# Attention and a cosine-gated feed-forward layer on one core: joint normalisation of two units in phases 3 to 5, with a newly searched order table

## The chip, the cores and the metric

The kernel runs on one core of a Trainium2 chip. Its time is the device time in microseconds (us) of one execution; the span is the part of it from the first to the last instruction in the trace. A core has five engines that run side by side and meet only at semaphores: PE (TensorE, matrix products into PSUM, with the weight load shown apart as PEld), DVE (VectorE), ACT (ScalarE), POOL (GpSimd) and SP (SyncE). In this kernel POOL and SP mostly issue transfers.

## The reference

The inputs are q, k and v of shape 8 x 8 x 576 x 64 (images, heads, positions, head width) and two weights, 512 x 2048 and 2048 x 512, all in float32.

```python
scores = scale * np.matmul(q, k.transpose(0, 1, 3, 2))       # scale = 1/8
bias = slopes[:, None, None] * (-np.abs(rel))[None, :, :]    # rel = position - position
mask = (rel >= 0) & (rel < 128)
attn = softmax(np.where(mask, scores + bias[None], -1e9))
x = np.matmul(attn, v)           # gathered to 4608 tokens x 512
h = x @ w_in
out = (h * np.cos(h)) @ w_out
```

## The kernel before

**Units.** Attention is cut into units: of each image (b), for two heads at a time (four pairs pr) and two halves of 256 positions (G = 0, 1), and one unit "t" for the last 64 positions of all heads: nine units an image, 72 in all. A unit has scores on PE (lines 529, 539), an exponential on ACT (590, 598), a product with the mask on DVE (611, 623) and a product with v on PE (640 to 656). The v tile has an added column of ones, so the last product also gives the sum by which the row must be divided. The norm is that division, on DVE: a reciprocal of the sums, and a product that writes 16-bit tokens, `xnats` (lines 694 and 696, function `norm`), out of the PSUM bank in which the v product stands. Afterwards the tokens are transposed into `xT`, either on PE and out of PSUM again (`x_pe`, lines 742, 752, 753) or by a transposing transfer from SP (`x_dma`, line 768). Units are handled two at a time; the v products of two units lie in PSUM banks 2 and 3.

**Two forms of norm.** Where both units of a group are ordinary ones and the phase is in the list `JN`, `norm_two` takes one reciprocal (line 710) and one product (line 712) over both banks together. Otherwise each unit has its own two instructions.

**Feed-forward.** The tokens are worked in nine chunks of 512. Chunk 0 multiplies by w_in in halves (975), chunks 1 to 5 with whole products (782), chunks 6 to 8 with sums of blocks that save one product in eight (876). The second product is plain in chunk 0 (1161) and in the block form from chunk 1 on (1067, 1138). The cosine is on ACT (787, 940, 980), its product with h on DVE (791, 943, 984).

**Phases and order.** Phase -1 has the nine units of image 0. Phases 0 to 5 stand beside the chunks of the same number and have 8, 10, 10, 12, 14 and 9 units. Every piece of work is recorded as an operation with its readers and writers; `Plan.follow` then unpacks a text, `TABLE`, into one sequence of all operations, and each engine and each queue runs its own operations in that sequence. The table also settles, where either is allowed, whether ACT or DVE copies something out of PSUM. Semaphore waits are derived from the readers and writers.

**Loads.** POOL issues the loads that change the type: q and k of images 0 and 1 in a row layout (356), v blocks (375), q and k of images 2 to 7 (385), w_in in four column quarters (407), w_out in four quarters (413). SP issues one first load of q, the transposing transfers of q and k of images 2 to 7 (396, 399), those of tokens (762, 768) and the stores of the output (1095, 1151, 1168). A load waits until its buffer is free, and what is behind it in its queue waits too.

**Start.** SP's first q load is cast by DVE and ACT (367, 368). POOL makes an identity matrix (420, 421) and the table of distances (427 to 434); ACT makes eight masks from the distances (460), and DVE widens them (465). PE transposes q and k of image 0 with the identity (483), in a first and a second part, and ACT and DVE copy them out (500, 501).

Of the kernel before, what the change touches and what calls it, by code (L numbers as in the profile page):

```python
# [8 lines left out]
ALU = mybir.AluOpType  # L9
# [5 lines left out]
B, H, S, D = 8, 8, 576, 64  # L15
NPAIR = H // 2
NBLK = 5
# [13 lines left out]
    'c-nPV2Y6If7JmPfH!Wo*A%PHdEHqifjs=k}tV#(GFqBXPBn4$bu`FK_%_4*%1ObV(K#D*JSt&-E!h-'  # L31
    '0xDvPKfD@{Z`QYO7kX6D^JciMYzU|;fHUhcd1+;jf_Kj&N_3_w#jJy552L+3%Pc;zlP#H-yktj(-'
    'pEjqM{ck}PJwCrB3q-'
    '{9M;&d$5qHR9WADS}~;_2H1xbO#`q+wdtgon`B>6%HyG|f?3%VnDsdnr<5N0St5ZZ)?8zmXNGD<Zg2=y6N`U+Gy?'
    '$F$*GyJWJoN!r+3anTS_iMU&FrmJy)q1{k##U*rYHRJHq^Dy35b!Y@oPU}o$A?_9;n<O%5Xs0l2&{m^^1BgNm_9P'
    '~pqObs4C1TN&{Qy{6(86~%nA#%H5NW^O=4`d2vLnc~h(_}2&mQcz_^`@$G{b79x#rnLjt-93Hcj0-'
    'yv%|m2e+*e0cZK}!+72b)WUaJT8@pXD+fk0N6bOV1gB(Si4?NA5T2-'
    '!JB(zEKr!Mj%{>;HUNYjab!Z7$qCql;L3G!CjefR+FFk(bw73vr<2ntCbb8MB)_5dQYyf6J%<J=0tY;ul(MgN&rc'
    'O0s&EiG$uIcm#Y~Vab;v#yqnaVrE7GY>V-A}Btqa`;P_Nv&jvF#{*7WM`>VMkre&#)Wy?uO_aV#gax-'
    'm{4=v5trFP6j>R?Tw2c0rY#J*M(j<PaOY>o)>#w^hUa2)xJ2kX>J~-'  # L40
    '#3SczLYEI#)13`0UMgZCvSU&r@KXVhQx8AYHOt^~S#t385v1pL)39f1&X4(!RY_VSn%~;N7Le~0Vt5k)3C!7qncH'
    'Sb_KKyP6<WQBL=(H{om`}^2hwehkBNkN1f6-'
    '=6Jf`#n1*9F&|{#~8ip5b`?XFO3>mnmKg4fqM&X#D2BXTu`vb#MxEL-'
    '2=FZh<=U!>)?uhVjo~ev?pC0h90j^d!W2#$W>Vg}3Lez;yMB~`dF58D5!*GHZ4bkokcrZJo8XMBIs3+J`c0!*&!='
    'cNak2M(+9t6%k<c;_TI5&xT-;_~SjMe)zLQ?kr-'
    '9G)}so_oZgT~!nS)>B%(>F{i(nL<%Kma6dPT_kIY8xqVGm@6sSZY)QY;}3kyZHF!JjrNbPWohF6A1kpQae^Jz>4Y'
    'nMq|4ag_#Z%abX$X0Qx{bdg5-'
    'w!C^Sy0wzSSv6YO*7!5g5KOZPW>L)jeqDWi^PVfHiNt_&bV&I7<#pb?el1f*R3lvbBscPqQM6(|M=#E!7MQtWiEo'
    '^$q8jetWg{{laSk`ID;w6<lHL!It@CI3ZRWxET-dy=6bdfZi^BN)-'
    'kx6rkxYh^Af7Y$CX%W0qP@nf!;+_cuy#JAV$$(>L5)aS8M@n1a32RRL3Yb{W0a`!VJ8|o4{JEnxs(L});p(&v8a9'  # L50
    'u_yO{KZHL$YuW?tu(Sy-'
    '!vCGTmAdZpg4wXLtycpkG<<E5@OtDZg=!_1h1+Njmjw*z0aL)7QnhFOPv(elHPlI>oe%EXgvk}suL+RHI+l!oPEe'
    'ttc)y)KY7q-'
    'GO9HpEp~!82*s>_!_J5TR{@5f%EL7h^Wh(4l4fbO%j~jd783&`#My06C4>3;+Is6L%3tT|^hYe#$tr1&iB&6{dwW'
    'wmj!;Baz_4=p8Jja_9ps>tY{=<;GUvOwSAXGq+K`;>!KNrH|ImXY(ASTzHFN^apdvpSj*r6^VK)$8H@P=`NPcPO&'
    'XkYSBhFw`irt0gqb!LQPqlVQC7VwU?z)4yP6n<)+6xUk=rH29r)HJ=#nkkufV0J5o_@v9wsQWd0@&P$WT0e*0vOC'
    'WIl=#9la*x}LDtWaQG=0xl2(#f%Kz3QWi+K|tR$xwKh#_K~ywPUk>V_~X988-'
    'dL$7M*|kTUzrMQ~>ttJm@GYT>9QFLiQ#JGHIu^Q5UX9joXGsV+1N~s5tf4rg&Z0t843@yK)VUZ;eO{vvf>bj#_<{'
    'E{YJE13lG{)N}UY3D6Y>lsCkRX4ja{$9_e$IQETy;j`zD56VwIGwJ{vRRhIkkY72;<?OL;WxyDsbjLJ`d?#gik4L'
    '%OwvOj>3X-Yk5pe`ia}jeHouYwjx-lYe?zUO*6w~{=z!E<7?VOdoJcyIBk3;YN22T&Udsl*?z2EoT*eN`VQ(2lOw'  # L60
    '$ie!%Cd#CND}y^H-5G~apWoVM#%(x$>q1=4UeA7@v$>FHVpXpRNz-`z1w9-2S&rNI|0<^yIkuIxJ1&2qr-'
    'yn-P&*BAkwbEg<YgZWM`B<Ux7!?;yxT0hEB9Poq9_H<xB+6$<+&1*V*jXQ=!i##UhbBC-HxJ9b4f>O5FQM$GVlYY'
    '0;EzOMeT$+Oi@ir?~G>em;QF`Fb7Uw0-'
    ')DSUv5QX5E;wvHsQX@ok50m+CO*%wR0XM0gH$JNq(o?|pd}rcrfU%@Ny^NS$EwY}9WNlRrb}CwAb0!CyUIkX8zeE'
    't`lBMNi5`Z9289jS-byN0#8`Z0-K46!6u51NJvfI*I<pVOKD}#Bep<(EjKAJ>#OvyA?}aT-'
    'Eb<QtZWG>gAiq@nZu|-Z>5YIIxXgTPJ-Qv8(%8OF{x~utj?J<T~4~q=Mu!G!`B%o{U^X7EYfMjy|cFw5l`KlR}P!'
    'Ka8_mW<8uzKs|eA|5Ic*_e7cdlcU3q+K^v!GU5I4-4igxj^A<ASLge=;<iQSZL!w7=WR?W#-'
    'vXhCLeN@7x(>g+{qRDABl6lLS<Fw>!h`LQKaFe(HMu)ipAva=P&;AW;|7_8}?>Xa&1&CWqRI3oTyJm0VHkMj~b-'
    'KU~R;VLVn(IO$x|2XD-#Cwa~YvoxGM@0FUnOnlZXB(9|3jhMQu{ARUV7(DVnyPJ@o)_f&pP-'
    '0v1&I@q5tK0fHEZqW2B6vpePz;Nsr3p!)OwvLraMQ%IB0%b!Fk8kvD!^ICX(d5SU`>)JBl;A)3x!^A~*gA1H!Njk'  # L70
    '9bb31AJ#9jLnSFn5nJP8V+>6WI*{{9$K=-'
    'Ii4(}ekB>9rlTbz8;dAV@$vsGY#Mm*p3)v9cI)0mEeyn;9Sk1Ej+_{IEB=6m(OWM%qp|L4FkV=POcUwRSz4?%tjO'
    '!EE7%nJVFo1y$1xLEKDW3+%V*`a_(LEi!<eA{Ja22J?)4@RI|7PRIIN8a6UkTIrQNx^0MmIX}Gdse33v8*ibI3(}'
    'Q6!`hQq7VFL0TWDyL%1z)LEb|Fqa2QJsRyz<9M$)jGC(Gyq6mu#GUiIyWiMn}lrw_vC^2CnX65Kq(JOA5auqsW#('
    'az6gPr;3Fs3vS*iFTO!lleCE-fW~K`s@;f-'
    'DuL7*vWwMFvwo)YDYK%Ys!&lL=}a$qa_Dqe_$j$%4|P%7Sk&C^p7|E-05OoaEoQU{w(_HKhuIl)N)0L6E?If-ndQ'
    'f>bOkomPRMj6=zXYB;2Fs8S$=8>KAS9bxj%$jo92RQykW$_h$ynL-'
    ';1n|B~0C{NjJ5M;#~HD{_qDyS92ASr8Q=(}$hf?wlN8Dh7U35CEE3Rb4eZHcVrLB=YO&ys+EVM&F9-'
    '>_E|awkyN8>TE$>Y^ZLfm%hXRv?#4)t*Y5EYzr4%5w1xWK3uw7gWYn<tfyI;9|8HRZ>;#t145fwkp%W<gb}oO8Vt'
    ';%~TDI391Zd3iT@kVuEmcuME+!AOkCeh?Xh408{MGRAGcvK=>2_;SOCz;Xi5FXBMh@##BcNK~)Hu608vNLvl*BDH'  # L80
    'GHNRFy;B3gs%n{7pj$fl+x7VWHhmHY6$LK<1t&5`BViq8BRfR0)!TR`@J<FZkbrVSDq@w=+*W79u-'
    'AsdYv9Vyey(st|R(RU84Bg0wsI(4aO|@>6G)${!)5eW-e@5K<&=Z_fWO<s>k5KMFa_g&GrXJ7L|{Z-'
    'kIjkN?mA0G*W>_y'
# [12 lines left out]
class Plan:  # L96
# [18 lines left out]
    def op(self, eng, fn, r=(), w=(), dma=None, occ=100, lat=None, pri=5, mode=0, table=None, two=False):  # L115
# [4 lines left out]
        f = fn[0] if isinstance(fn, list) else fn["act"] if isinstance(fn, dict) else fn  # L120
# [39 lines left out]
    def follow(self, text):  # L160


        raw = zlib.decompress(base64.b85decode(text))
        n, at, self.order = len(raw) // 2, 0, []
        assert n == len(self.all)
        for lo, hi in zip(raw[:n], raw[n:]):
            at = (at + lo + 256 * hi) % 65536
            o = self.all[at % 32768]
            if isinstance(o.fn, dict):
                e = "dve" if at >= 32768 else "act"  # L170
                o.fn, o.eng = o.fn[e], (e,)
            self.order.append(o)
# [80 lines left out]
def bass_alibi_sliding__then__act_gcu_kernel(  # L253
# [8 lines left out]
    with ExitStack() as ctx:  # L262
# [12 lines left out]
        JN, PRE2, SEEDN, XD, LORD = (5,), (), {}, {4: 6}, 0  # L275
# [583 lines left out]
        def moe1_fast(c, f4):  # L859
# [76 lines left out]
            def gk(hf):  # L936
                return [("g", gi, 4 * f4 + k, hf) for k in range(4)]

            def cos_and_product(src, srcs, o, cos, occ, w, r, ck, hf):
# [3 lines left out]
                op("dve", lambda e: e.tensor_tensor(o, srcs, cos, ALU.mult),  # L943
                   r=r + ck, w=w + gk(hf), occ=1139, lat=1225, pri=MPRI, two=hf == 1)
# [272 lines left out]
        distances()  # L1217
        identity()
        load_qk("q", q, 0, 1)
        load_qk("k", k, 0, 1)  # L1220
        constants()
        load_v(0, range(2))
        load_w_in(0)
        load_v(0, range(2, NBLK - LORD))
        masks()
        for n in range(2):
            qk_transposes(0, "q", n, 0, OB)
            qk_transposes(0, "k", n, 0, UB)
        for u in range(1, 4):
            load_w_in(u)  # L1230
            if u == 1:
                load_v(0, range(NBLK - LORD, NBLK))
# [92 lines left out]
```

## Time and profile before

| | |
|---|---|
| median of 3 runs (lowest, highest) | 300.07 us (299.7, 300.19) |
| the profiled execution | 299.71 us, of which 298.0 us is the span |
| granted TensorE clock in it | 1.000 |
| PE busy, share of the span | 287.9 us, 97% |
| PEld busy | 205.2 us, 69% |
| DVE busy, instructions | 262.1 us, 88%, 522 |
| ACT busy, instructions | 222.1 us, 75%, 318 |
| POOL busy | 95.2 us, 32% |
| chain that ended last, by engine | PE 94% |

Busy time is the time in which at least one instruction of the engine runs. Matrix products are pipelined: one that takes 0.38 us is followed by the next after 0.22 us, so their busy times overlap, and a short stop of PE can be hidden in them. It is seen in the distance between the starts of two products.

### The profile page before, as it was taken

The numbers are of one execution on the slowest core, as the hardware profiler recorded it, in microseconds if no ns is written. First come the engines' busy times: TensorE is split into PE (matmuls) and PEld (weight loads), VectorE is DVE, ScalarE is ACT, GpSimd is POOL, SyncE is SP. The second block draws the span as 40 slices with busy tenths as digits, with TensorE's granted clock in tenths as the row PEclk, the third lists the DMA queues.
The fourth block names the chain that finished last, engine by engine and source line by source line (L and its number), as shares of the span: only waits on it lengthen the run. The fifth ranks groups of instructions, "written<-read, shape, count | busy, mean of one in ns | idle before, by whom it ended". The sixth has DMA issues, their size and how long they took to land.

```text
span 298.0 us, 7278 instructions
## 1 busy us (share of the span) xinstructions
PE 287.9 (97%) x2974; PEld 205.2 (69%) x2974; DVE 262.1 (88%) x522; ACT 222.1 (75%) x318; POOL 95.2 (32%) x122
## 2 busy tenths in 40 slices
PE   2899999999999999999999999999999999999996
PEld 2678845446874586458854788547768888888884
DVE  3879877599977999899999999999999999999972
ACT  5788878689757889688777878579778758778620
POOL 7997000599642303991195005000000000000000
PEclk9999999999999999999999999999999999999999
DMA  7999999999999994999999939973131400041033
GB/s 153 173 205 208 207 169 146 180 196 155 136 175 147 130 187 90 142 173 173 169 170 133 163 85 130 159 164 74 21 79 21 150 2 0 2 141 37 10 134 106
DMA packets 147729, 37.96 MB, mean 127 GB/s; under 512 B 133360, under 2 KB 146416, under 8 KB 147696
## 3 DMA queue, kind: packets, MB, share of 16 engines
q0 software_dynamic: 99344, 18.10, 79.7%
q1 hardware_dynamic: 48352, 19.41, 34.5%
q8 instruction: 23, 0.38, 0.5%
q14 instruction: 10, 0.08, 0.1%
HBM read 36.70 MB, written 9.44 MB: 155 GB/s over the span
## 4 chain that ended last, share of the span: by engine, by line
PE 94%; DVE 2%; POOL 1%; issue 1%; ACT 1%; POOLq 0%; DVEq 0%
PE ps L1067 33%; PE ps L782 24%; PE ps L876 11%; PE ps L539 5%; PE ps L975 5%; PE ps L1161 4%; PE ps L653 3%; PE ps L656 2%; PE ps L742 2%; PE ps L483 2%; PE ps L529 1%; DVE kt L501 1%; PE ps L640 1%; PE ps L642 1%; PE ps L1138 1%
## 5 line engine op out<-in xcount | busy, mean ns | idle before, releaser
L1067 PE MATMUL ps<-w_outb,gT 128*128 128x256 f16 x512 | 82.3, 273 | 0.0
L782 PE MATMUL ps<-xT,w_inb 128*128 128x512 f16 x336 | 82.2, 379 | 0.0
L787 ACT ACTIVATE cos<-ps,halfpi 128x512 f32<-128x512 f32 x84 | 54.9, 687 | 18.9 <-PE ps L782 13.9
L598 ACT ACTIVATE p<-ps 128x768 bf16<-128x768 f32 (+1 forms) x64 | 55.6, 915 | 11.5 <-PE ps L539 9.5
L791 DVE TENSOR_TENSOR gT<-ps,cos 128x512 f16<-128x512 f32 x84 | 54.5, 686 | 5.5 <-ACT cos L787 5.1
L1067 PEld LDWEIGHTS ps<-w_outb,gT 128*128 128x128 f16 x512 | 48.2, 98 | 12.5 <-issue 1.3
L782 PEld LDWEIGHTS ps<-xT,w_inb 128*128 128x128 f16 x336 | 31.7, 98 | 31.1 <-DVE gT L791 1.5
L375 POOL DMA_DIRECT2D vp<-in_v_dram x40 | 34.3, 892 | 53.1 <-PE ps L656 35.3
L1067 PE MATMUL ps<-wsum,gsum 128*128 128x256 f16 x256 | 38.5, 273 | 0.0
L623 DVE TENSOR_TENSOR p<-p,emask 128x768 bf16<-128x768 bf16 (+1 forms) x64 | 38.0, 615 | 0.3
L385 POOL DMA_DIRECT2D qnat<-in_q_dram x30 | 25.5, 918 | 23.9 <-DMA qt<-qnat 23.9
L1052 ACT ACTIVATE ob<-ps 128x512 f32<-128x512 f32 x33 | 19.6, 598 | 13.7 <-PE ps L1067 11.2
L385 POOL DMA_DIRECT2D knat<-in_k_dram x30 | 25.7, 948 | 9.3 <-DMA kt<-knat 7.0
L1067 PEld LDWEIGHTS ps<-wsum,gsum 128*128 128x128 f16 x256 | 23.2, 98 | 4.0 <-issue 0.5
L876 PE MATMUL ps<-xT,w_inb 128*128 128x256 f16 x132 | 24.8, 273 | 0.0
L696 DVE TENSOR_TENSOR xnats<-ps,rec 128x256 f16<-128x256 f32 x56 | 21.9, 420 | 0.5
L539 PE MATMUL ps<-qt,kt 64*128 64x128 bf16 (+1 forms) x320 | 20.1, 253 | 1.3 <-DVE kt L501 1.3
L653 PEld LDWEIGHTS ps<-vp,p 128*128 128x128 bf16 x256 | 16.0, 99 | 4.3 <-issue 1.0
L653 PE MATMUL ps<-vp,p 128*128 128x65 bf16 x256 | 18.9, 196 | 0.1
L1067 PE MATMUL ps<-wsum,gT 128*128 128x256 f16 x112 | 18.1, 273 | 0.0
L539 PEld LDWEIGHTS ps<-qt,kt 64*128 64x128 bf16 x320 | 11.9, 98 | 8.6 <-issue 3.6
L1161 PE MATMUL ps<-w_outb,gT 128*128 128x512 f16 x64 | 17.6, 380 | 0.0
(111 smaller groups left out, 478.0 us busy)
## 6 DMA issues: line engine op xcount, KB each, us to landing
out_dram<-ob SPq DMA_DIRECT2D x35, 256.0 KB, 2.7
vp<-in_v_dram POOLq DMA_DIRECT2D x32, 128.0 KB, 6.9
qnat<-in_q_dram POOLq DMA_DIRECT2D x24, 128.0 KB, 7.1
knat<-in_k_dram POOLq DMA_DIRECT2D x24, 128.0 KB, 10.8
w_inb<-in_moe_w_in_dram POOLq DMA_DIRECT2D x4, 512.0 KB, 10.5
w_outb<-in_moe_w_out_dram POOLq DMA_DIRECT2D x4, 512.0 KB, 21.8
gsum<-in_q_dram POOLq DMA_DIRECT2D x1, 576.0 KB, 15.5
gsum<-in_k_dram POOLq DMA_DIRECT2D x1, 576.0 KB, 17.6
```

Source lines behind the costliest of these rows:

```text
L375: op("pool", [lambda e, t=t, rows=rows: e.dma_start(vp[b % 2][0:rows, t, :, 0:64], v[b, :, 128 * t:128 * t + rows, :].rearrange("h p d -> ...
L385: fns.append(lambda e, t=t, rows=rows: e.dma_start(nat[which][b % 2][0:rows, t, :, :], src[b, :, 128 * t:128 * t + rows, :].rearrange("h p ...
L539: ins = e.matmul(ps[:, banks[x], c0:c1], keys_ap(b, x, pr, kc), query_ap(b, x, pr, qb, 128 * nb), start=c0 == 0 and (b, pr, G) not in seed ...
L598: op("act", lambda e: e.activation(P[i][:, :, 0:hi], src_[:, :, 0:hi], ACTF.Exp, scale=0.125), w=held + [("P", i)], occ=920 if G else 691, ...
L623: op("dve", lambda e: e.tensor_tensor(p, p, m, ALU.mult), r=[("EM", h0), ("EM", h1)] + ([] if G else [("EM2", h1)]), w=[("P", i)], occ=600 ...
L653: ins = e.matmul(o, P[i][:, x, d0:d0 + 128], V[:, kc, h, 0:65], start=True, stop=not two)
L782: op("pe", lambda e, kc=kc: e.matmul(ps[:, bank, :], w_in[:, kc, 128 * fc:128 * fc + 128], xT[:, kc, r0:r0 + CH], start=(kc == 0), stop=(k ...
L787: op("act", lambda e: e.activation(cosb[ci][:, :], ps[:, bank, :], ACTF.Sin, bias=halfpi[:, 0:1]), r=["halfpi"], w=[("B", bank), ("cos", c ...
L791: op("dve", lambda e: e.tensor_tensor(gT[gi][:, fc, :], ps[:, bank, :], cosb[ci][:, :], ALU.mult), r=[("cos", ci)], w=[("B", bank), ("g", ...
L876: op("pe", lambda e, i=i, kc=kc: e.matmul(ps[:, bank, 256 * i:256 * i + 256], left(kc, p0 + i), right(kc), start=(start and i == 0 and kc ...
L1067: op("pe", lambda e, t=t, p=p: e.matmul(ps[:, bank, 256 * t:256 * t + 256], left(p, slice(128 * t, 128 * t + 128)), right(p), start=(start ...
L1161: op("pe", lambda e, t=t, fc=fc, bank=bank: e.matmul(ps[:, bank, :], gT[gi][:, fc, 128 * t:128 * t + 128], w_out[:, fc, :], start=(fc == 0 ...
```

## The change

1. `JN` goes from `(5,)` to `(3, 4, 5)`: the norms of two ordinary units are taken together in phases 3 and 4 too. There are five such groups in each, so ten groups go from four DVE instructions to two. The pair numbers are rounded up to even ones, so some tokens land in another of the eight `xnat` buffers.
2. `TABLE` is another text, with a new sequence for all operations, searched with transfers in which the two queues (POOL's and SP's) hold each other up.
3. Two options are added and stay off: `LORD == 3` (`LORD` stays 0), an order of the first loads, and `PCOS` (false), one product of chunks 6 to 8 on POOL. With both off they add no instruction.

Unpacked, the new table differs so: PE has the same 2974 instructions; DVE has 499 instead of 522 (20 norms fewer, three copies given to ACT net), ACT three copies more. Of PE's 1860 recorded operations 1018 stand in a common order with the old table, of POOL's 70 there are 39, of SP's 86 there are 48. The work of a unit and of a chunk stays in its phase; the order within it moves.

- Start, POOL: the second q load and the second k load go ahead of most of the distance work, and the identity ahead of the last two distance instructions (the distances then end last); the first two v blocks change places. From the first v block to entry 27 POOL's list is the same: v, w_in quarters, q and k of image 1, w_out quarters, v of image 1, q of image 2.
- Start, ACT and DVE: ACT begins with the cast of q and makes five masks before the first copy, where the old list had two masks, the cast and four more masks. Of the second part's copies of k, both were on DVE; now one is on ACT. PE's scores of the third unit stand before the second part's transposes of k, and the scores of the eighth unit before two of the first four token transposes. Ahead of the first product with the fourth w_in quarter (`moe1_half`, line 975) stand 49 such products and six token transposes, where there were 50 and seven.
- Later, POOL: one v block of image 2 goes between q and k of image 2; q of image 5 and k of image 7 go ahead of several v blocks.
- Later, SP: the first block of image 4 (`x_dma`) stands behind a store of chunk 2; k of image 4 stands ahead of a store of chunk 1 and of the tail tokens of image 2; the first store of chunk 3 stands ahead of k of image 6.
- The end: PE's last 128 products (the second product of chunk 8), and the last five stores, stand in nearly the same order.
- Phases 3 and 4: counted in PE's list with each product at its usual step in the trace, the time from the end of the v products of two units to the next use of one of their banks by other work is shortest, in the new list, for four pairs that get a joint norm: 1.2 us each (units (4,1,1) with (4,2,1), (5,0,0) with (5,1,0), (5,2,0) with (5,3,0), (5,2,1) with (5,3,1), written image, pair, half). In the old list the same four have 1.4, 1.4, 1.0 and 1.6 us.

```diff
 TABLE = (
-    'c-nPV2Y6If7JmPfH!Wo*A%PHdEHqifjs=k}tV#(GFqBXPBn4$bu`FK_%_4*%1ObV(K#D*JSt&-E!h-'
...
+    'c-n1N2|!d;8+`|6m<<>PoIzBi&BV-d$t7D%!c>+3Wl=-~2?Rv}5lt~cEkzN6Ko-FjG(>O#6)SBs_4n6GtxPM?&>x'
...
 )
@@ Plan.op
-        f = fn[0] if isinstance(fn, list) else fn["act"] if isinstance(fn, dict) else fn
+        f = fn[0] if isinstance(fn, list) else next(iter(fn.values())) if isinstance(fn, dict) else fn
@@ Plan.follow
-                e = "dve" if at >= 32768 else "act"
+                e = "dve" if at >= 32768 else o.eng[0]
@@ settings
-        JN, PRE2, SEEDN, XD, LORD = (5,), (), {}, {4: 6}, 0
+        JN, PRE2, SEEDN, XD, LORD = (3, 4, 5), (), {}, {4: 6}, 0
+        PCOS = False
@@ cos_and_product
-                op("dve", lambda e: e.tensor_tensor(o, srcs, cos, ALU.mult),
-                   r=r + ck, w=w + gk(hf), occ=1139, lat=1225, pri=MPRI, two=hf == 1)
+                f = lambda e: e.tensor_tensor(o, srcs, cos, ALU.mult)
+                if hf and PCOS:
...
+                else:
+                    op("dve", f, r=r + ck, w=w + gk(hf), occ=1139, lat=1225, pri=MPRI,
+                       two=hf == 1)
@@ first loads
+        if LORD == 3:
...
+        else:
+            distances()
+            identity()
...
```

More of the change, by code (lines that the diff above doesn't have):

```diff
@@ L38 @@
[L38 to L66, printed above, removed]
@@ L1216, in bass_alibi_sliding__then__act_gcu_kernel @@
         load_qk("k", k, 0, 0)
[L1217 to L1232, printed above, removed]
+        if LORD == 3:
+            distances()
+            load_v(0, range(2))
+            identity()
+            load_w_in(0)
+            load_qk("q", q, 0, 1)
+            load_qk("k", k, 0, 1)
+            constants()
+            masks()
+            load_w_in(1)
+            load_v(0, range(2, 4))
+            load_w_in(2)
+            load_w_in(3)
+            load_v(0, range(4, NBLK))
+            for n in range(2):
+                qk_transposes(0, "q", n, 0, OB)
+                qk_transposes(0, "k", n, 0, UB)
+        else:
+            distances()
+            identity()
+            load_qk("q", q, 0, 1)
+            load_qk("k", k, 0, 1)
+            constants()
+            load_v(0, range(2))
+            load_w_in(0)
+            load_v(0, range(2, NBLK - LORD))
+            masks()
+            for n in range(2):
+                qk_transposes(0, "q", n, 0, OB)
+                qk_transposes(0, "k", n, 0, UB)
+            for u in range(1, 4):
+                load_w_in(u)
+                if u == 1:
+                    load_v(0, range(NBLK - LORD, NBLK))
         load_qk("q", q, 1)
```

79 lines of the change are left out of this document (56 added, 23 removed).

## The prediction

> **What bounds the kernel now.** I read the page's shares first, then the chain that ended last, then stretches of the span, then the distances between starts on PE.
>
> ```profile
> PE 287.9 (97%) x2974; PEld 205.2 (69%) x2974; DVE 262.1 (88%) x522; ACT 222.1 (75%) x318; POOL 95.2 (32%) x122
> PE 94%; DVE 2%; POOL 1%; issue 1%; ACT 1%; POOLq 0%; DVEq 0%
> ```
>
> PE is busy nearly always and carries 94% of the chain; everything else together holds some 18 us of it. Where is that? Three stretches (columns: PE, PEld, DVE, ACT, POOL busy us):
>
> ```profile
> 0.00:18.00 18.00, 11.03 (x161) 8.55 (x162) 12.07 (x36) 13.25 (x23) 16.42 (x29) 1.00 1.24 170
> 18.00:280.00 262.00, 261.83 (x2682) 184.12 (x2681) 239.51 (x472) 204.93 (x289) 78.76 (x94) 1.00 1.20 126
> 280.00:298.00 18.00, 15.09 (x136) 12.51 (x134) 10.51 (x16) 3.89 (x6) 0.00 (x0) 1.00 0.31 103
> ```
>
> PE lacks 7.0 us in the start, 2.9 us at the end, and 0.17 us in the 262 us between. Busy time hides short stops, so I went through the starts of the products one by one.
>
> ```profile
> 190.76 8.63 PE ps L782 x40
> ```
>
> ```profile
> 51.62 0.38 PE L1161 MATMUL ps<-w_outb,gT 128*128 128x512 f16 x1
> 52.04 0.19 PE L653 MATMUL ps<-vp,p 128*128 128x65 bf16 x1
> ```
>
> Forty products in 8.63 us are 0.216 us each: the usual step of a 512-column product. At 51.62 the next start comes after 0.42, so 0.2 us are lost; that is one of the three largest losses there are after 18 us. Summed over all neighbours after 18 us, counting what a step takes beyond the shortest step of the same two forms, I get 2.4 us. So the middle could give back 2.4 us at the very most, and each us that DVE or a queue saves there is worth nothing unless it ends one of those stops.
>
> **The change, part by part.**
>
> *Ten joint norms.* Durations:
>
> ```profile
> L696 DVE TENSOR_TENSOR xnats<-ps,rec 128x256 f16<-128x256 f32 x56 | 21.9, 420 | 0.5
> L694 DVE RECIPROCAL rec<-ps 128x4 f32<-128x4 f32 x56 | 7.6, 169 | 7.6 <-PE ps L656 7.1
> L712 DVE TENSOR_TENSOR xnats<-ps,rec 128x512 f16<-128x512 f32 x4 | 2.7, 684 | 0.0
> L710 DVE RECIPROCAL rec<-ps 128x8 f32<-128x8 f32 x4 | 0.8, 204 | 0.3 <-PE ps L656 0.2
> ```
>
> A pair costs 2 x (420 + 169) = 1178 ns now and 684 + 204 = 888 ns joint: 290 ns less, 2.9 us over ten pairs. But DVE starts an instruction before the last has ended:
>
> ```profile
> 172.34 0.25 DVE L694 RECIPROCAL rec<-ps 128x4 f32<-128x4 f32 x2
> 172.51 0.66 DVE L623 TENSOR_TENSOR p<-p,emask 128x1024 bf16<-128x1024 bf16 x1
> 173.09 0.42 DVE L696 TENSOR_TENSOR xnats<-ps,rec 128x256 f16<-128x256 f32 x1
> 173.43 0.68 DVE L623 TENSOR_TENSOR p<-p,emask 128x1024 bf16<-128x1024 bf16 x1
> ...
> 208.67 0.20 DVE L710 RECIPROCAL rec<-ps 128x8 f32<-128x8 f32 x1
> 208.78 0.51 DVE L623 TENSOR_TENSOR p<-p,emask 128x768 bf16<-128x768 bf16 x1
> 209.21 0.68 DVE L712 TENSOR_TENSOR xnats<-ps,rec 128x512 f16<-128x512 f32 x1
> 209.81 0.55 DVE L623 TENSOR_TENSOR p<-p,emask 128x768 bf16<-128x768 bf16 x1
> ```
>
> By steps, two reciprocals take 0.17 us and each product 0.34: 0.85 a pair. Joint it is 0.11 + 0.60 = 0.71. DVE gains 0.14 a pair, 1.4 us in all. On the path: nothing, since PE runs beside it without a stop. If PE were not full there, these 1.4 us would be the price. The three copies that go to ACT (0.3 to 0.4 us each for token copies) lie beside PE too; ACT is 75% busy.
>
> *Banks.* A joint product frees both banks only at its end, while the first of two single products frees one of them earlier. Counted along PE's lists, four pairs in phases 3 and 4 have 1.2 us between the end of their v products and the next use of a bank, where the old lists leave 1.4, 1.4, 1.0 and 1.6. The norm chain of a joint pair is 208.67 to 209.89 above, 1.22 us with a mask product in between, and 0.20 + 0.68 = 0.9 us without. So each of these four places loses between nothing (DVE at hand) and 0.3 us (DVE half of a 0.60 step late): 0 to 1.2 us in all. Below nothing it could only be by ending stops that are there now, and those are in the 2.4 us. I take 0.1: DVE often comes first and waits for PE, as the 7.1 us behind line 694 show, though mostly in early phases.
>
> *Start.* The old order of the copies after the first and the second part of the transposes:
>
> ```profile
> 6.81 0.60 ACT L500 ACTIVATE qt<-ps 128x512 bf16<-128x512 bf16 x1
> 10.57 0.88 ACT L500 ACTIVATE qt<-ps 128x640 bf16<-128x640 bf16 x1
> 12.07 1.51 ACT L598 ACTIVATE p<-ps 128x768 bf16<-128x768 f32 x2 [0.62 <-PE ps L539]
> ...
> 11.79 1.57 DVE L501 COPY kt<-ps 128x640 bf16<-128x640 bf16 x2
> 13.50 1.04 PE L539 MATMUL ps<-qt,kt 64*128 64x256 bf16 x12 [0.38 <-DVE kt L501]
> 17.39 0.64 PE L529 MATMUL ps<-qt,kt 64*128 64x64 bf16 x16
> ```
>
> DVE copies two parts of k one after the other, and PE's scores at 13.50 wait for the second. In the new lists one is ACT's. There the third unit's exponential can start after the copy of q (10.57 + 0.74 = 11.3) because its scores now precede the transposes of k; it steps 0.75 us, so the copy of k runs from 12.05 to 12.9 and the scores start at about 13.05 instead of 13.50. The exponentials behind them move up by about 0.5 us, and the tail scores, which wait for the exponential before the last, by 0.55: 16.85 instead of 17.39. One product of chunk 0 (0.11 us) is then already done. That is 0.65 us sooner at equal work. Against it: the distances end last, so five masks of 0.31 us come after about 5.5 us and may hold the first copy from 6.81 to 7.2, 0.4 us later. What is late next is w_in:
>
> ```profile
> L407 POOL DMA_DIRECT2D w_inb<-in_moe_w_in_dram x4: 782/794/800, 8.2 to 11.3; - x4
> DMA to landing us min/median/max: 7.9/10.5/13.2
> 24.42 0.60 PE L975 MATMUL ps<-xT,w_inb 128*128 128x256 f16 x4
> ```
>
> The fourth quarter lands at 11.3 + 13.2 = 24.5; its first user is the fourth of the four at 24.42, at 24.75. The new list has one product and one token transpose less ahead of it, 0.11 + 0.11 us. With the start at 24.5 PE then stands where it would stand at 24.7 now, so whatever the start gains, only about 0.05 us survive, unless w_in lands sooner. POOL issues as much ahead of it as before, so I keep 24.5. Bounds -0.65 (loads come sooner, too) and +0.4; I take -0.1, near the cap.
>
> *POOL and SP lists.* No row of the wait list has PE behind a transfer, so nothing is to be gained; the loss is a landing past its use. How long transfers take (60 to 100 us, then 185 to 235 us, when POOL's queue is almost empty):
>
> ```profile
> kt<-knat SPq DMA_TRANSPOSE x4, 10.5
> ...
> kt<-knat SPq DMA_TRANSPOSE x2, 4.0
> ```
>
> The queues do hold each other up. The tightest now is the last v block of image 4, and the first block of image 4's tokens moves most:
>
> ```profile
> 133.24 1.73 POOL L375 DMA_DIRECT2D vp<-in_v_dram  x2
> vp<-in_v_dram POOLq DMA_DIRECT2D x1, 64.0 KB, 14.1
> 148.33 0.19 PE L640 MATMUL ps<-vp,ptail 128*128 128x65 bf16 x1
> 121.91 1.39 SPq L768 DMA_TRANSPOSE xT<-xnats  x1
> xT<-xnats SPq DMA_TRANSPOSE x1, 7.2
> 148.95 1.24 PE L782 MATMUL ps<-xT,w_inb 128*128 128x512 f16 x5
> ```
>
> The v block lands at 147.3, 1.0 us ahead. In the new list q of image 5 has left the queue long before it and it stands one place sooner: safer. The token block waits behind a store whose data PE finishes at about 134.5; issued at 136, it lands at 143 and is used at 148.5. What stands behind that store in SP (a store, then tokens ready at 143) is not hurried. The first store of chunk 3, now ahead of k of image 6, has its data by about 142. I take 0; one late transfer would cost up to its own lateness, some 1 us from these rows.
>
> *End.* Same order: 0.
>
> **Sum:** 299.71 (span 298.0 and 1.7 around it) + 0.1 - 0.1 = 299.7. This execution is 0.36 below the median of 300.07, so for the median I say 300.1.
>
> **Rivals.**
>
> *A, the start keeps its gain:* w_in lands early with the earlier q and k loads, and 0.65 us survive: 299.4. For it: the DVE wait at 13.50. Against: the 24.5 landing.
>
> *B, DVE is the bound.* DVE is busy 239.5 of 262 us, and if PE's fullness is only overlap, its 1.4 us come through: 298.7. Against it stands the 0.216 step. The weight loads of those products:
>
> ```profile
> L782 PEld LDWEIGHTS ps<-xT,w_inb 128*128 128x128 f16 x336 | 31.7, 98 | 31.1 <-DVE gT L791 1.5 <-ACT xT L752 0.8 <-DVE xtail L684 0.4
> ```
>
> The Trainium skill, in Perfetto Trace Analysis, Identifying the Most-Contended Engine, says that matmul busy time misjudges PE's headroom and weight-load busy time should be used; by that rule PE is at 69%, DVE at 88% is the most contended engine, and the sum would be B's. By that rule, the trace does not agree: a load of 98 ns lies inside each step of 0.216 us, so PE can be full with its loads at rest half the time.
>
> *C, slower: banks come free too late.* In phases 3 and 4, at the four pairs with 1.2 us, DVE is 0.3 us late each: +1.2, 301.3. It decides from 0.15 late at each (0.6). For it: DVE at 96% there,
>
> ```profile
> 150.00:185.00 35.00, 35.00 (x394) 24.17 (x393) 33.61 (x76) 27.33 (x36) 15.27 (x19) 1.00 1.65 137
> PEld ps L742 <- DVE xnats L696: 2.4, 9, 0.4
> ```
>
> and PE's weight loads already wait behind norms. Against: the phase-5 joint norms are waited for in no row.
>
> **Numbers.** 0.2%, 0.6 us, is about what a measurement of this kernel can tell from no change. No measurable change 0.45 (299.5 to 300.7, likeliest 300.1); A 0.15; B 0.08; C 0.32. A lies just across the bound, so faster 0.23, same 0.45, slower 0.32. The range from 299.2 to 301.3 leaves out B and the far end of C.
>
> **What would show it.** Right: PE still lacks under 0.5 us between 18 and 280; line 710 x14, DVE about 2.9 us less busy; the w_in rows and the fourth quarter's first product near 24.5. A: that product before 24.2. B: PE's distances shrink in 150 to 280. C: waits of PE for line 712. Wrong altogether: PE behind a transfer, above all behind k of image 6 or tokens of image 4.

## The result, and the profile after

The changed kernel takes 300.91 us (300.0 to 301.58), the kernel before beside it on the same chip 300.12 (299.56 to 300.5). The ratio is 1.0029, with a 95% interval of 1.0021 to 1.0037: 0.8 us slower, just past the 0.2% that I took for what can be told from no change. Its profiled execution took 300.85 us, its span 299.1.

Busy times, and the chain that ended last by engine, from the page of the changed kernel:

```profile
PE 288.2 (96%) x2974; PEld 203.7 (68%) x2974; DVE 258.9 (87%) x499; ACT 223.3 (75%) x321; POOL 95.3 (32%) x122
...
PE 91%; DMA 5%; POOL 3%; issue 1%; ACT 0%; POOLq 0%
```

DVE is 3.2 us less busy and PE about as full as before, but 5% of the chain now runs through transfers, where there were none. The two stretches that answer to those of before (columns: PE, PEld, DVE, ACT, POOL):

```profile
0.00:18.00 18.00, 10.95 (x169) 8.01 (x170) 11.00 (x36) 14.00 (x24) 16.50 (x29) 1.00 1.23 165
18.00:280.00 262.00, 260.94 (x2663) 182.29 (x2662) 236.08 (x448) 204.25 (x291) 78.77 (x94) 1.00 1.19 126
```

In the first 18 us PE already starts 169 instructions where there were 161: the start is faster. Between 18 and 280 us PE lacks 1.06 us instead of 0.17, and has started 19 instructions fewer. The rows of the wait list that are new, with the row of the joint products (columns: total us, times, longest):

```profile
PEld ps L983 <- DMA w_inb<-in_moe_w_in_dram: 1.6, 3, 0.9
...
PEld ps L655 <- DVE xnats L714: 0.9, 3, 0.5
...
PE ps L983 <- DMA w_inb<-in_moe_w_in_dram: 1.0, 2, 0.8
```

(Lines stand 2 to 8 higher in the changed kernel: 983 are chunk 0's products, 655 and 658 the v products, 714 the joint product, 698 the single one, 744 the token transposes on PE, 784 and 1075 the products of the later chunks.) PE now waits for w_in, 1.0 us in two stops, and its weight loads wait for joint products. From the timelines of PE and of PEld, the longest of the stops on w_in and the one at the fourth quarter:

```profile
20.02 1.70 PE L983 MATMUL ps<-xT,w_inb 128*128 128x256 f16 x14 [0.77 <-DMA w_inb<-in_moe_w_in_dram]
```

```profile
25.13 0.66 PEld L983 LDWEIGHTS ps<-xT,w_inb 128*128 128x128 f16 x7 [0.33 <-DMA w_inb<-in_moe_w_in_dram]
```

The longest stands at the second quarter, which landed at 19.97 us (19.40 before), not at the fourth, for which the prediction had worked out its cap.

**Where the loss stands.** Busy time hides stops of 0.1 us, so I place them with a worked measure. Each PE instruction gets its usual step from the trace of before (a low quarter of the distances to the next start, form by form); the steps added up are the work done; the *lag* is how much later another trace reaches the same work. The changed kernel's lag is -0.92 us at 19 us (ahead), +0.62 at 26, +0.28 at 62, +0.78 at 140, +1.07 at 280. PE ends 1.24 us later. So three things happen: a lead of 0.9 in the start that is more than lost at w_in, some 0.5 us lost from 62 to 140 us, where no norm was changed, and some 0.3 us in phases 3 to 5.

In the start this measure has a fault: the execution of before that it is taken from is itself late there. From PE's timelines of before and of a kernel with the same start (old start, new rest, in the table below):

```profile
15.83 1.22 PE L742 MATMUL ps<-ident,xnats 128*128 128x128 f16 x8
...
17.39 0.64 PE L529 MATMUL ps<-qt,kt 64*128 64x64 bf16 x16
```

```profile
15.60 0.40 PE L744 MATMUL ps<-ident,xnats 128*128 128x128 f16 x4
...
17.11 0.41 PE L531 MATMUL ps<-qt,kt 64*128 64x64 bf16 x16
```

PE's products still take longer in before: eight transposes 1.22 us, where the other does four in 0.40, and 16 small products 0.64 where they take 0.41. The first record of the granted clock (1.00) stands at 17.93 us in that trace, at 14.30 in the other and at 13.54 in that of the changed kernel, and PE's products get shorter about there; what sets that time no run here shows. All other traces with the old start begin these 16 products between 16.89 and 17.11 us and stand 0.50 to 0.71 us ahead of before at 19 us; those with the new start, 0.82 to 1.15. So the order of the start itself is worth some 0.4 us (the means are 0.55 and 0.96), and the rest of the lead belongs to that one execution.

The theories that went into the runs: **T1**, w_in comes too late and eats the start's gain; **T2**, the joint norms cost by banks that come free late; **T3**, the finer order of everything behind chunk 0 costs. They share one table of results, ratios against the kernel before on the same chip (a ratio need not be the quotient of two medians):

| kernel | median us | ratio, 95% interval | fourth w_in quarter lands | lag at 62 | 62 to 140 | 140 to 280 |
|---|---|---|---|---|---|---|
| before | 299.9 to 300.1 | 1 | 24.48 | 0 | 0 | 0 |
| changed | 300.91 | 1.0029, 1.0021 to 1.0037 | 25.09 | +0.28 | +0.50 | +0.29 |
| new start, old rest | 300.46 | 1.0025, 1.0001 to 1.0049 | 24.66 | -0.16 | +0.25 | -0.02 |
| old start, new rest | 301.22 | 1.0032, 1.0018 to 1.0047 | 23.80 | -0.38 | +0.56 | +0.15 |
| old order, joint norms | 300.93 | 1.0017, 0.9997 to 1.0037 | 24.18 | -0.30 | -0.02 | +0.50 |
| new order, split norms | 302.35 | 1.0073, 1.0055 to 1.0092 | 24.57 | -0.03 | +0.50 | +1.87 |
| new order, old first POOL entries | 300.94 | 1.0025, 1.0012 to 1.0039 | 25.31 | +0.49 | +0.47 | +0.43 |
| new order, first w_in quarter only | 300.41 | 1.0012, 0.9999 to 1.0024 | 24.65 | -0.03 | +0.48 | +0.69 |
| old order, first w_in quarter only | 299.50 | 0.9989, 0.9975 to 1.0003 | 24.72 | -0.51 | -0.01 | -0.02 |
| new start, old POOL entries, old rest | 300.23 | 1.0006, 0.9993 to 1.0020 | 24.60 | +0.40 | +1.09 | -0.03 |
| new order, 73 to 93 us old | 301.06 | 1.0030, 1.0016 to 1.0043 | 24.18 | -0.64 | +1.09 | +0.15 |
| old order, 73 to 93 us new | 301.62 | 1.0055, 1.0036 to 1.0074 | 24.74 | +0.26 | +1.35 | +0.14 |
| old to 140 us, new behind | 303.44 | 1.0108, 1.0084 to 1.0132 | 24.19 | +0.13 | +0.02 | +3.07 |
| new order, v products of phases 3 to 5 later | 301.36 | 1.0044, 1.0031 to 1.0057 | 24.96 | +0.31 | +0.48 | +0.82 |

The last four columns (us) describe one profiled execution of each, the median many. The profiled execution can be a quick one: that of the old start with the new rest took 300.02, 1.2 us below its median.

### The profile page after: what moved, and what is told of

The parts are those of the page before. It is cut to its first block, busy times and chain, and to the rows that moved or that the text cites. A ratio compares the mean times of both kernels' runs of the same rounds, so it can differ in the third digit from the quotient of the medians.

```text
span 299.1 us, 7255 instructions
## 1 busy us (share of the span) xinstructions
PE 288.2 (96%) x2974; PEld 203.7 (68%) x2974; DVE 258.9 (87%) x499; ACT 223.3 (75%) x321; POOL 95.3 (32%) x122
## 4 chain that ended last, share of the span: by engine, by line
PE 91%; DMA 5%; POOL 3%; issue 1%; ACT 0%; POOLq 0%
PE ps L1075 33%; PE ps L784 24%; PE ps L878 11%; PE ps L1169 5%; DMA w_inb<-in_moe_w_in_dram 5%; PE ps L541 5%; PE ps L983 3%; PE ps L655 3%; PE ps L658 2%; PE ps L744 1%; POOL vp L377 1%; PE ps L485 1%; PE ps L642 1%; POOL gsum L358 1%; PE ps L531 1%
## 5 line engine op out<-in xcount | busy, mean ns | idle before, releaser
L784 PE MATMUL ps<-xT,w_inb 128*128 128x512 f16 x336 | 83.2, 379 | 0.0
L878 PE MATMUL ps<-xT,w_inb 128*128 128x256 f16 x132 | 25.3, 273 | 0.0
L1075 PE MATMUL ps<-wsum,gT 128*128 128x256 f16 x112 | 19.5, 273 | 0.0
L655 PE MATMUL ps<-vp,p 128*128 128x65 bf16 x256 | 18.6, 195 | 0.3 <-DVE p L625 0.2
L658 PE MATMUL ps<-vp,p 128*128 128x65 bf16 x192 | 17.3, 194 | 0.0
L983 PE MATMUL ps<-xT,w_inb 128*128 128x256 f16 x128 | 16.3, 273 | 1.0 <-DMA w_inb<-in_moe_w_in_dram 1.0
## 6 DMA issues: line engine op xcount, KB each, us to landing
qnat<-in_q_dram POOLq DMA_DIRECT2D x24, 128.0 KB, 11.2
w_inb<-in_moe_w_in_dram POOLq DMA_DIRECT2D x4, 512.0 KB, 11.2
```

What stands on the lines that cost most here:

```text
L655: ins = e.matmul(o, P[i][:, x, d0:d0 + 128], V[:, kc, h, 0:65], start=True, stop=not two)
L784: op("pe", lambda e, kc=kc: e.matmul(ps[:, bank, :], w_in[:, kc, 128 * fc:128 * fc + 128], xT[:, kc, r0:r0 + CH], start=(kc == 0), stop=(k ...
L878: op("pe", lambda e, i=i, kc=kc: e.matmul(ps[:, bank, 256 * i:256 * i + 256], left(kc, p0 + i), right(kc), start=(start and i == 0 and kc ...
L1075: op("pe", lambda e, t=t, p=p: e.matmul(ps[:, bank, 256 * t:256 * t + 256], left(p, slice(128 * t, 128 * t + 128)), right(p), start=(start ...
```

## The experiments

In all of them TABLE was written anew, so the diffs show the list that it stands for.

### Which part of the order costs: start or rest

```diff
 operations 1 to 551 (to the end of chunk 0, about 62 us)
-old order
+new order
 operations 552 to 2842: old order, single norms
```

> The first 551 operations stand in the new order (up to the end of chunk 0, about 62 us, the loads issued in that time with them), all later ones in the old order with single norms. T1 (the loss stands in the start: w_in lands 0.57 us later and the gain of the start is eaten): slower than before by 0.5 to 0.9 us, the whole difference. T2 (the ten joint norms cost, by banks that come free later): within 0.2 us of before. T3 (the finer order of everything behind chunk 0 costs): by the lag of 0.28 us that the new kernel has at 54 to 62 us, about 0.3 us slower than before. I hold T3 with that share of T1.

```diff
 operations 1 to 551: old order
 operations 552 to 2822
-old order, single norms
+new order, ten joint norms
```

> The mirror: the first 551 operations in the old order, all later ones in the new order with the ten joint norms. T1: as before, within 0.2 us. T2 and T3: 0.5 to 0.9 us slower than before; T2 would have the stops behind the joint norms in phases 3 and 4 alone, T3 spread from 72 us on.

The old start with the new rest has the whole loss (1.0032), so T1 isn't needed for it. The new start with the old rest stands at 1.0025 with an interval from 1.0001 to 1.0049, which tells little by itself: by time, either half alone costs about as much as both. Its lag is -0.16 at 62 us, and 0.25 us then come in behind the seam of the two orders. The lag from 62 to 140 us is the firmer number: +0.47 to +0.56 in all six kernels that have the new order throughout from 62 to 140 us, and within 0.02 of nothing in the three that have the old one there without a seam. It repeats to 0.1 us, while medians carry 0.4.

### The joint norms alone, and taken out

```diff
 phases 3 and 4, old order, each of ten pairs
-reciprocal a, product a, reciprocal b, product b
+reciprocal a and b, product a and b   (at the place of the earlier)
```

> The old order everywhere, and only the ten pairs of norms of phases 3 and 4 made joint, each at the place of the pair's earlier norm. T2: 0.5 to 0.9 us slower than before, with stops of PE behind the joint product. T1 and T3: within 0.3 us of before. DVE should be about 2.9 us less busy; the rival that DVE is the bound would have it 1.4 us faster, 298.7.

```diff
 phases 3 and 4, new order, each of ten pairs
-reciprocal a and b
+reciprocal a, product a
-product a and b
+reciprocal b, product b
```

> The new order everywhere, with the ten joint norms of phases 3 and 4 split into the old single ones, one unit's pair at the place of the joint reciprocal and the other's at the place of the joint product. T2: back to the time of before, or most of the way. T1 and T3: within 0.3 us of the changed kernel, 0.5 to 1.1 us slower than before.

In the old order the joint norms show no gain: 1.0017, and DVE, 261.1 us busy, has 1.0 us less, nearer to the 1.4 counted by steps than to the 2.9 of the durations. So DVE's work was not what bounds the kernel, and rival B falls. The medians stand 0.9 us apart and the interval reaches to 1.1 us, so T2's 0.5 to 0.9 us slower is not excluded here; the trace, of one of the quickest executions (300.21), loses 0.50 in two stops of 0.3 us. One of them, first on DVE, then on PE's weight loads:

```profile
152.77 0.21 DVE L712 RECIPROCAL rec<-ps 128x8 f32<-128x8 f32 x1 [0.24 <-PE ps L658]
153.08 0.69 DVE L714 TENSOR_TENSOR xnats<-ps,rec 128x512 f16<-128x512 f32 x1
```

```profile
153.82 0.33 PEld L784 LDWEIGHTS ps<-xT,w_inb 128*128 128x128 f16 x3 [0.51 <-DVE xnats L714]
```

The products of chunk 4 want a bank that the joint product holds to 153.77. This is the pair (5,2,0) and (5,3,0), for which I had counted 1.0 us in the old list, the shortest of the four. The other stop, 0.29 at 143.86, is token transposes that wait for a joint product (0.40).

In the new order the split norms are much worse: 1.0073, and 1.87 us lost from 140 to 280 us. I had put that kernel within 0.3 us of the changed one (T1, T3) or near the time of before (T2); all were wrong. The largest stop, on DVE and on PE's weight loads:

```profile
186.31 0.18 DVE L694 RECIPROCAL rec<-ps 128x4 f32<-128x4 f32 x1
186.59 0.42 DVE L696 TENSOR_TENSOR xnats<-ps,rec 128x256 f16<-128x256 f32 x1
```

```profile
187.07 0.10 PEld L653 LDWEIGHTS ps<-vp,p 128*128 128x128 bf16 x1 [0.67 <-DVE xnats L696]
```

Norm, mask product and norm take 1.9 us there, from 185.09 to 187.01, and PE needs both banks; reciprocal, mask product and joint product of the same pair take 1.6 in the changed kernel (183.96 to 185.58). So the cost of a norm on DVE does reach PE, 1.3 us over ten pairs, when the list on PE was laid out for the shorter one. T2 as I had put it (joint norms cost, single ones do not) holds for the old order, if anywhere, and is reversed in the new one: each list fits the norms that it was made with.

### What makes the start lose its lead

```diff
 POOL, new order
-k, q, distances, k, identity, identity, distances, distances
+k, distances, q, distances, distances, k, identity, identity
```

> The changed kernel, with POOL's first eight entries (three row loads, three distance instructions, two of the identity) back in the old order; all else new. So far the fourth w_in quarter landed at 24.48, 23.80 and 24.18 us with the old start and at 25.09, 24.66 and 24.57 with the new. T1a (the earlier row loads make w_in late): it lands at 24.2, give or take 0.3, PE waits for it less, and the kernel is 0.3 to 0.6 us faster than the changed one, so 0.3 to 0.6 slower than before. T1b (they do not; the landing is chance or comes from something else): it lands at 24.6 to 25.1, and the time is that of the changed kernel, 0.6 to 1.1 us slower than before.

The order of the first loads shows no effect (T1a falls): with the old one w_in landed later still, at 25.31, and the time is that of the changed kernel. The rows of the w_in load, of that kernel and of the changed one with the stretch from 73 to 93 us old, whose POOL entries are the new ones:

```profile
L409 POOL DMA_DIRECT2D w_inb<-in_moe_w_in_dram x4: 782/798/803, 8.1 to 11.2; - x4
...
  PE ps L983: 1.3, 2
...
DMA to landing us min/median/max: 7.4/11.3/14.1
```

```profile
L409 POOL DMA_DIRECT2D w_inb<-in_moe_w_in_dram x4: 782/794/800, 8.1 to 11.2; - x4
...
  PEld ps L983: 0.8, 3
...
DMA to landing us min/median/max: 7.4/10.3/13.0
```

Both issue the fourth quarter at 11.2; it lands 14.1 and 13.0 us later. So the landing differs from one execution to the next by more than the change could move it: 23.80 to 24.74 with the old start (six executions, mean 24.35), 24.18 to 25.31 with the new (eight, mean 24.75). Whether the new start itself adds the 0.4 between these means is open.

The lag at 62 us follows the landing. Among the seven new starts that multiply by all of w_in it is -0.64, -0.03, -0.16, +0.31, +0.28 and +0.49 for landings at 24.18, 24.57, 24.66, 24.96, 25.09 and 25.31 (the seventh, at 24.60, has +0.40). Where w_in landed at 24.18, 0.64 us were left of a lead of 0.96 at 19 us; where it landed after 25 all was gone. From the second on, the quarters land some 2.5 us apart, so a late fourth quarter goes with a late second one: the second landed between 19.22 and 20.20 us in these seven.

```diff
 moe1_half, chunk 0, in both orders
-w_in[:, kc, 128 * fc:128 * fc + 128]               reads ("wi", fc // 4), ("wia", fc // 4)
+w_in[:, kc, 128 * (fc % 4):128 * (fc % 4) + 128]   reads ("wi", 0), ("wia", 0)
```

> The changed kernel, with one part of the computation changed: chunk 0 multiplies by the first quarter of w_in's columns four times instead of by the four quarters, so none of its products waits for quarters two to four. T1 (the arrival of w_in eats the start's gain): the stops of 0.93, 0.35 and 0.22 us on it go, the lead of 0.6 us at 18 us is still there at 30 us, and the kernel is 0.9 to 1.4 us faster than the changed one: between 0.5 faster and equal to before. Rival (PE has something else to wait for there, a bank or a copy): less than 0.5 us of that.

> The kernel before, with the same change of the computation: chunk 0 uses the first quarter of w_in's columns four times. By the prediction the old list meets the fourth quarter as it lands, at 24.5 to 24.75, and loses next to nothing: within 0.3 us of before. Rival (the old list is held by w_in as well, and its start of 0.65 us later is hidden behind it): 0.4 to 0.7 us faster.

With the new order the lead is 1.15 us at 19 us and still 1.14 at 26: the stops on w_in were T1's, as expected. Then it is lost at the next load. From the timeline of PE in that kernel:

```profile
26.83 0.38 PE L983 MATMUL ps<-xT,w_inb 128*128 128x256 f16 x2
27.99 0.75 PE L485 MATMUL ps<-ident,gsum 128*64 128x128 bf16 x20 [0.78 <-DMA gsum<-in_q_dram]
```

PE stops 0.78 us until q of image 1 has landed, its weight loads wait for k as well, and the lag is back at -0.24 by 30 us, -0.03 at 62. I had expected the lead to last and the kernel to gain 0.9 to 1.4 us; it gained some 0.5. POOL's queue of loads paces PE beyond w_in: taking one wait away shows the next. The old order gains 0.5 us from the same edit by its median (0.9989, an interval that just takes in 1). By the median that is the rival's forecast, by the ratio, 0.3 us, it lies at the edge of the other. The traces with the old start lean to the rival: behind 19 us the second quarter of w_in costs nothing in one (old start, new rest), 0.2 us in the old order with joint norms, and 0.5 and 0.8 in the two with old order to 140 us and with 73 to 93 us new. In the execution that the prediction read it cost nothing: PE came to it at 19.44, just behind its landing at 19.40. Beside that execution this kernel's lead is 0.71 us already at 19 us, ahead of any stop on w_in, so the -0.51 at 62 us is not a price of w_in.

```diff
 operations 1 to 551, POOL's first eight entries
-new order
+old order
 the rest of 1 to 551: new order;  552 to 2842: old order
```

> The first 551 operations in the new order but POOL's first eight entries in the old one, and all behind that in the old order with single norms: what would beat both kernels if the new start is good but for the row loads. T1a: w_in lands at 24.2, give or take 0.3, and the time is 0.2 to 0.6 us below before. T1b: as the earlier kernel with the new start and the old rest, between equal and 0.5 us slower than before.

At 1.0006 it is as fast as the kernel before; the 0.2 to 0.6 us of T1a are not there. Its profiled execution lost 0.85 us in one stop between two v products at 83.83 that no other trace has, and for which the profile names no releaser.

### The stretch from 73 to 93 us

From 82 to 89 us the last units of image 2 pass through two banks in a chain: v products, norm, transposes, copy, next v products. Counted in PE's operations, the new list leaves 6, 6, 3 and 6 from one link to the next where the old one has 7, 7, 4 and 7. Weight loads that waited there, of the changed kernel and of before:

```profile
84.87 0.10 PEld L655 LDWEIGHTS ps<-vp,p 128*128 128x128 bf16 x1 [0.18 <-ACT xT L754]
...
85.84 0.10 PEld L1075 LDWEIGHTS ps<-wsum,gT 128*128 128x128 f16 x1 [0.37 <-DVE ob L1130]
...
86.39 0.11 PEld L744 LDWEIGHTS ps<-ident,xnats 128*128 128x128 f16 x2 [0.33 <-DVE xnats L698]
...
87.16 0.10 PEld L655 LDWEIGHTS ps<-vp,p 128*128 128x128 bf16 x1 [0.21 <-ACT xT L754]
...
88.38 0.11 PEld L744 LDWEIGHTS ps<-ident,xnats 128*128 128x128 f16 x2 [0.32 <-DVE xnats L698]
```

```profile
83.31 0.11 PEld L742 LDWEIGHTS ps<-ident,xnats 128*128 128x128 f16 x2 [0.21 <-DVE xnats L696]
...
85.91 0.11 PEld L742 LDWEIGHTS ps<-ident,xnats 128*128 128x128 f16 x2 [0.25 <-DVE xnats L696]
...
86.67 0.10 PEld L653 LDWEIGHTS ps<-vp,p 128*128 128x128 bf16 x1 [0.21 <-ACT xT L752]
...
87.89 0.11 PEld L742 LDWEIGHTS ps<-ident,xnats 128*128 128x128 f16 x2 [0.32 <-DVE xnats L696]
```

PE loses 0.09 to 0.11 us at four of the five in the new list (all but 85.84) and as much at two places without a row, 0.61 us from 82 to 89; in the old list it is 0.23 at two. That is 0.38 of the 0.5. Three of the four stand at links that are one operation shorter (84.87, 86.39, 88.38); the link of three operations has no stop. Ahead of 87.16 both lists have as many operations between transposes and v products, but those of the new list take 0.1 us less.

```diff
 operations 639 to about 756, all engines
-new order
+old order
```

> The changed kernel with some 120 operations (from 73 to 93 us, the end of the attention units of image 2) back in the old order; start, joint norms and all the rest new. Between 80 and 90 us the new list has 6, 6, 3 and 6 of PE's operations between a group of v products and the transposes that need their norm, or between transposes and the v products that need their bank, where the old list has 7, 7, 4 and 7; and five kernels with the new order there lost 0.5 to 0.7 us between 72 and 95 us. Theory (bank turnover one product too short): that loss falls below 0.2 us, the stops of 0.1 us ahead of v products and transposes go, and the kernel is 0.4 to 0.6 us faster than the changed one, 0.2 to 0.5 slower than before. Rival (the loss belongs to DVE's load and moves elsewhere): the same lag by 100 us, time of the changed kernel.

```diff
 operations 639 to about 760, all engines
-old order
+new order
```

> The mirror: the kernel before with only that stretch of about 120 operations in the new order. Theory (bank turnover): 0.4 to 0.7 us slower than before, lost between 80 and 95 us in stops of about 0.1 us ahead of v products and transposes, nothing after. Rival: within 0.2 us of before.

The stretch itself behaves as expected. In the old kernel the new stretch has the same five waits at the same distances:

```profile
84.74 0.10 PEld L653 LDWEIGHTS ps<-vp,p 128*128 128x128 bf16 x1 [0.18 <-ACT xT L752]
...
85.72 0.10 PEld L1067 LDWEIGHTS ps<-wsum,gT 128*128 128x128 f16 x1 [0.37 <-DVE ob L1122]
...
86.27 0.11 PEld L742 LDWEIGHTS ps<-ident,xnats 128*128 128x128 f16 x2 [0.33 <-DVE xnats L696]
...
87.03 0.10 PEld L653 LDWEIGHTS ps<-vp,p 128*128 128x128 bf16 x1 [0.21 <-ACT xT L752]
...
88.25 0.11 PEld L742 LDWEIGHTS ps<-ident,xnats 128*128 128x128 f16 x2 [0.32 <-DVE xnats L696]
```

But as a measurement of its price both runs failed. The seams cost more than the stretch: 0.36 us at 80.86 and later stops of 0.26 and 0.36 where the stretch went back to the old order, 0.64 at 92.34 and 0.34 at 134.51 where it went to the new. So the kernel that should have gained 0.4 to 0.6 us gained nothing (1.0030), and the mirror lost 1.6 instead of 0.4 to 0.7. That the order of this stretch makes the stops is shown both ways: with the new list they stand in the old kernel too, and with the old list in the changed kernel there are two again, at 83.21 and 85.81. That the shorter distance is what does it is read from the waits, not tested alone; that widening the distances would win 0.4 us is not shown.

### The change of phases 3 to 5 by itself

```diff
 operations 1 to 1182 (to about 140 us): old order
 operations 1183 to 2822
-old order, single norms
+new order, ten joint norms
```

> The old order for the first 1182 operations (up to about 140 us) and the new order for all later ones, with the ten joint norms: the change of phases 3 to 5 by itself, as the search arranged it. By the lag of the kernel with the old start and the new rest (0.18 at 140 us, 0.32 at 290) it is 0.1 to 0.3 us slower than before. Rival C of the prediction (four joint pairs hold their banks 0.3 us too long each): 1.2 us slower, in stops behind the joint product. Rival B (DVE is the bound): 1.4 us faster.

It is 3.4 us slower, and 3.0 of it is one stop behind the seam of the two orders. From the timelines of DVE and of PE:

```profile
158.32 0.69 DVE L819 TENSOR_TENSOR qnat<-w_inb 128x1024 f16<-128x1024 f16 x1 [3.38 <-DMA qt<-qnat]
```

```profile
160.28 1.04 PE L784 MATMUL ps<-xT,w_inb 128*128 128x512 f16 x4 [2.40 <-DVE gT L793]
```

A sum of weights that is written into the buffer of q waits until the transposing transfer of q has read it. Here the transfer came late: it was issued at 145.59, 0.6 us sooner than in the changed kernel, but its two parts landed at 156.66 and 158.23 instead of 150.76 and 151.59, and why is open. DVE stood 3.38 us, the products behind it in DVE's list stood too, and PE waited for their banks. Apart from that stop, the lag moves by less than 0.15 us from 140 to 280, as expected, but the time says nothing on the change. It prices what the prediction put at nothing: one late transfer can cost 3 us, not 1.

```diff
 PE's list, phases 3 to 5, new order
-v products of the tail unit of image 4
+the same, two operations later
-v products of five groups behind joint norms
+the same, one operation later
```

> The changed kernel, every engine's list as it is but for PE's in phases 3 to 5: the v products of the tail unit of image 4 come two of PE's operations later, those of five more groups behind joint norms one operation later (0.1 to 0.2 us each). Of the stops that the changed kernel has and the old one has not, three stand there: 0.17 us at 149.15, 0.14 at 187.78, 0.14 at 214.67; at 187.78 the weight load waits 0.46 us for the joint product. Theory (rival C of the prediction in small: a joint norm frees its bank 0.1 to 0.2 us too late for the next v products): the three stops fall below 0.05 each, and between 140 and 290 us the kernel loses 0.3 to 0.45 us less than the changed one, which also is what the median should gain, 300.5. Rival (DVE's load is what is short, so the wait moves to the next group): the stops turn up elsewhere and the time is that of the changed kernel.

In the changed kernel, the joint product and the weight load at 187.8, from the timelines of DVE and of PEld:

```profile
187.03 0.69 DVE L714 TENSOR_TENSOR xnats<-ps,rec 128x512 f16<-128x512 f32 x1
```

```profile
187.77 0.10 PEld L655 LDWEIGHTS ps<-vp,p 128*128 128x128 bf16 x1 [0.46 <-DVE xnats L714]
```

Ended at 187.72, waited for until 187.77: the bank is the cause. For the stops at 149.15 and 214.67 the profile names no releaser. With the v products one operation later the stops at 187.78 and 214.67 are gone, as the theory says. Others came: 0.51 at 149.60, where PE's row names an exponential on ACT (line 600) and no norm, and this one, of 0.29 on PE:

```profile
155.07 0.10 PEld L784 LDWEIGHTS ps<-xT,w_inb 128*128 128x128 f16 x1 [0.51 <-DVE xnats L714]
```

The second fits the theory: moved v products make their own norm later, and the next user of the bank meets that: the same pair (5,2,0) and (5,3,0) as in the old order with joint norms. The kernel lost 0.82 us from 140 to 280 where the changed one lost 0.29. By time the rival was nearer: the wait moved, in part to ACT.

No kernel here is faster than the one before by more than its interval.

## Why the prediction was right, and where it was wrong

I said 300.1 with a range of 299.2 to 301.3; it is 300.9 beside 300.1. The range holds it. The likeliest case, no measurable change, does not, by a little: 0.8 us slower against a bound of 0.6.

*Norms, nothing on the path: right.* DVE lost 3.2 us of busy time and PE gained nothing; the joint norms alone in the old order made nothing faster, so B did not hold. The Trainium skill, in Perfetto Trace Analysis, Identifying the Most-Contended Engine, judges PE by weight-load time and by the share of its peak work that it does (MFU); the prediction's rival took the first alone. By that half of the rule DVE at 88% against 69% of weight loads had to be relieved; the trace does not agree, since 1.0 us less of DVE gave no time back. But "nothing" on the path is one-sided. The split norms in the new order cost 1.3 us beside the changed kernel: an engine that is not the bound still delays PE when its instruction is the one a bank waits for.

*Banks, +0.1: right in mechanism, too small.* Weight loads wait for joint products as C said, 0.14 to 0.3 us a stop, in the old order at one of the four named pairs, in the changed kernel also at others. The changed kernel lost 0.29 from 140 to 280 us, the other executions of the same list between 0.15 and 0.69, so a third of C's 1.2 would have been the better value. Of the three largest stops in the changed kernel, 0.17, 0.14 and 0.14, the profile puts one down to a joint product.

*Start, -0.1: the cap was right, the gain was in part luck.* The tail scores started at 16.83, worked out as 16.85. But the scores behind the copies of k started at 13.33, not at 13.05, and the 17.39 that the 16.85 was set against is that of a late execution: against 17.11 of the same start elsewhere the gain is 0.28, and 0.4 with the product already done, not 0.65. W_in took it, as the cap said, but most of it at the second quarter, which the prediction did not look at. "I keep 24.5" was the weak step: one execution was taken for a fixed time, and landings spread from 23.8 to 25.3. On average new and old start are level at 62 us: a lag of +0.09 over the seven new ones with all of w_in, -0.06 over the five old ones.

*Lists of POOL and SP, 0: right.* Behind 31 us no row of the changed kernel has PE behind a transfer. *End, 0:* 0.06 us from 280 to 290.

*What failed* is a sentence of the part on banks: that four pairs in phases 3 and 4 are where turnover gets tight. I counted these distances only where norms are joined. The loss of 0.5 us from 62 to 140 us is the same mechanism in phase 1, with single norms, where the new list is one PE operation shorter at four links. In the sum it had no term at all. The old trace had a sign of it, two stops of 0.1 us in the same chain, one of them at one of these links. The 2.4 us that the prediction gives for all such stops does not come out as it is described: against the shortest step of the same two forms the neighbours behind 18 us add up to some 14 us, most of it in hundredths; against the usual step, stops of 0.05 us and more add up to 2 us.

## What to carry to other kernels

- Where an engine is full, count the distance of every turnover of a shared buffer, in both lists, not only where the instructions change. One operation of 0.1 to 0.2 us less went with a stop at three of four links here.
- A gain ahead of a load is worth what the load's landing leaves, and a landing is a spread: here 1.5 us wide over executions with nearly the same issue time. The same holds for PE's pace in a start: a gain read from one execution can belong to that execution.
- A list that was searched as a whole can't be tested in pieces by time alone. Seams cost 0.3 to 3 us here, more than the pieces; a lag at equal work, read per stretch, told 0.1 us.

## What was not expected of the hardware

- The same four loads, issued within 0.3 us of the same time, landed between 23.80 and 25.31 us (fourth quarter). Within a load, the first and the last of its shares landed 1.1 to 2.4 us apart.
- A joint product can wait for a transfer. It writes two token buffers at once, and one may still be read by a token transfer. In two of the seven traces with the new order in phase 4 the wait list has the row; of the new order with the first w_in quarter only, timeline of DVE:

```profile
184.96 0.69 DVE L714 TENSOR_TENSOR xnats<-ps,rec 128x512 f16<-128x512 f32 x1 [0.52 <-DMA xT<-xnats]
```

PE lost 0.49 us behind it, and 0.07 in the changed kernel at the same place. The prediction's list of waits did not have this one; it may be part of why the changed kernel's times spread 1.6 us and those of before 0.9, which no run here settles.
